# The second gate-and-up tile made whole instead of in two halves, in a hand-ordered stage

## The chip, the cores and the metric

The kernel runs on one core of a Trainium2 chip. The metric is the device time of one execution in microseconds (us), the median of several runs.

## What is computed

An input x of 2048 rows and 512 columns goes through two blocks, each behind a layer norm and with a residual. The first filters in the frequency domain, the second is a gated feed-forward network with 1376 hidden columns:

```python
def _A_ref(x, w_r, w_i):
    X = jnp.fft.rfft2(x, axes=(-2, -1))
    X = X * (w_r + 1j * w_i)
    return jnp.fft.irfft2(X, s=(S, D), axes=(-2, -1))

def _B_ref(x, w_gate, w_up, w_down):
    g = jnp.einsum("bsd,df->bsf", x, w_gate)
    u = jnp.einsum("bsd,df->bsf", x, w_up)
    return jnp.einsum("bsf,fd->bsd", _gelu(g) * u, w_down)

h = x + _A_ref(_layernorm(x), A_w_r, A_w_i)
h2 = h + _B_ref(_layernorm(h), B_w_gate, B_w_up, B_w_down)
```

## The kernel before

The Fourier transforms are matrix products with tables of cosines and sines. The 2048 rows are 16 blocks b of 128. The first part (lists START and SECOND in the code) transforms there, filters, and goes back over one axis. The stage changed here is written out by hand in the list FIRST: every name in it issues one step, and each engine works off its own steps in the order of the list. It finishes the way back for blocks 0 to 7, prepares them for the second block of the network, and makes the first two tiles of gate and up. Behind it the loop over `gate_up(n)` makes the other tiles, mixed with the products of w_down (`fill`).

The second block works in tiles: n counts (half of the rows, 128 hidden columns), and a tile's 512 columns are the rows of four pairs of blocks, (0,4), (1,5), (2,6) and (3,7), 128 columns of each block's transposed parts. Gate and up are multiplied by a scheme of seven products P0 to P6 in place of eight, and every product is done as three of high and low parts, over two halves of the contraction: six matmuls for one product, whatever its width. A tile has three PSUM banks x, y, z: 0, 1, 2 for even n, 3, 4, 5 for odd n. x takes P0, P2, P4, P5; y takes P1; z takes P3, P6.

The letters of the list, with the engine and the line of its work:

- On the way back for a block b: u, w, U (TensorE, L527: four matmuls, u and w two each), C (ACT, L853 for blocks 0 to 7, L820 for 8 to 15), V (DVE, L861; for block 3 GpSimd, L859), X (GpSimd, L884), M (TensorE, L866), O (ACT, L871), H (DVE, L876: residual), G and I (GpSimd, L880), S and A (DVE, L517 and L519: statistics). K (GpSimd, L827 to L830) unfolds a late block; U and C of blocks 8 to 15 are later needed.
- For a pair i: E (DVE, L898), Q (ACT, L911: reciprocal root), N (DVE, L903 to L905: its Newton step), R (ACT, L909: scaling, R20 is pair 2, first block), T (TensorE, L560 and L566: four transposes, T20 needs R20).
- The parts of a pair, from the transposes: s, e (ACT copies, L571 and L579), c, d, h (DVE differences, L582), k (GpSimd, L582), and the high parts a, f, i, l, n (ACT, L585) with their low parts b, g, j (DVE), m, o (GpSimd, all L588). Products P0 and P1 read a and b, P2 and P3 read f and g, P4 reads n and o, P5 reads i and j, P6 reads l and m.
- For a tile: P0 to P6 (TensorE, L163 to L165), c1, c2, c3 (ACT copies of x, L670), d1, d2, dy (DVE additions, L673), G0, G1 (ACT, L676: gelu), m0, m1 (DVE, L679: times), i0, i1 (ACT, L685: high), o0, o1 (DVE, L692: low). wh and wl load w_down (ACT and GpSimd). Tile 0 is g0, tile 1 is g1, its halves of 256 columns a and b: g0bP2 is product P2 of the second half of tile 0. g2P0 is the first product of tile 2, on bank 0, which ends the list.
- r0 to r3 (GpSimd), hc (DVE, L223) and lo1 to lo3 (GpSimd, L228) prepare the weights of tile 2.

The number behind a dot is a PSUM bank or a buffer (U15.3: bank 3, T21.7: bank 7, K9.5: row buffer 5). Waits between engines are set by the framework in the order of the list.

Of the kernel before, what the change touches and what calls it, by code (L numbers as in the profile page):

```python
# [62 lines left out]

SECOND = """
# [55 lines left out]
def kernel(  # L120
# [18 lines left out]
    o3 = out[: S // 2].rearrange("(p b) d -> p b d", b=NB // 2)  # L139
# [37 lines left out]
    k3 = ctx.enter_context(tc.tile_pool(name="k3", bufs=1))  # L177
# [57 lines left out]
    with (  # L235
# [176 lines left out]
        wh = cp.tile([P, NT, 2, 2, 2], F32, name="wh")  # L412
# [216 lines left out]
    def products(n, i=slice(0, 4)):  # L629

        w, at = gu[tiles[n][1]], slice(i.start * P, i.stop * P)

        x, y, z = places = [ps[:, 5 if k == 2 and n >= NF else 3 * (n % 2) + k, at] for k in range(3)]

        def product(o, wm, m, onto=False):
            def do():
                mm3(
                    o,
                    [
                        (  # L640
                            (w[:, 0, wm, c], w[:, 1, wm, c]),
                            tuple(cb[:, h, m, c, i].rearrange("p i n -> p (i n)") for h in range(2)),
                        )
                        for c in range(2)
                    ],
                    onto,
                )
# [12 lines left out]

    def tile_of(n, i=slice(0, 4)):

        at = slice(i.start * P, i.stop * P)
        (x, y, z), by_pe = products(n, i)
        if n not in sums:
            sums[n] = sum_tiles()
        s1, u2, u3 = (t[:, at] for t in sums[n])

        def copy(to, a):
            return lambda: act.activation(to, a, AF.Copy)  # L670

        def add(to, a, b):
            return lambda: dve.tensor_tensor(to, a, b, op=ALU.add)  # L673

        def gelu(g):
            return lambda: act.activation(g, g, AF.Gelu_apprx_tanh)  # L676

        def times(u, g):
            return lambda: dve.tensor_tensor(u, u, g, op=ALU.mult)  # L679

        def high(k, u):
            def do():
                if n not in parts_of:
                    parts_of[n] = w3.tile([P, 2, 2, 512], F32R, name="a", bufs=3)
                act.activation(parts_of[n][:, 0, k, at], u, AF.Copy)  # L685

            return do

        def low(k, u):
            def do():  # L690
                a = parts_of[n][:, :, k, at]
                dve.tensor_tensor(a[:, 1], u, a[:, 0].bitcast(F32), op=ALU.subtract)  # L692
# [99 lines left out]
    def sum_tiles():  # L792
        return [w3.tile([P, 512], F32, name=f"s{k}") for k in range(1, 4)]
# [11 lines left out]
    do = {}  # L805
# [84 lines left out]
    def pair(i):  # L890

        bs, where = slice(i, i + 5, 4), []
        r = rs2[:, bs]
        hn = [spare[1 + i // 2][:, 2 * (i % 2) + h] for h in range(2)]

        def eps_added(k):
            where.append(k)
            dve.tensor_scalar(ps[:, k, 0:2], mv2[:, bs, 1], EPS, None, op0=ALU.add)  # L898

        def newton():  # L900

# [3 lines left out]
            dve.scalar_tensor_tensor(r, t, 1.5, r, op0=ALU.add, op1=ALU.mult)  # L905

        def normed(h):
            b = i + 4 * h
            return lambda: act.activation(hn[h], gh[:, b], AF.Copy, scale=rs2[:, b : b + 1])  # L909
# [517 lines left out]
```

## Time and profile before

| what | us |
| --- | --- |
| timed runs: median of 3 | 440.44 |
| timed runs: lowest, highest | 440.41, 441.14 |
| the profiled execution | 440.5 |
| its span, first to last instruction | 438.6 |
| TensorE busy, of the span | 432.0 |
| DVE and GpSimd busy, of the span | 314.2 and 314.5 |
| ACT busy, of the span | 243.1 |

The clock granted to TensorE was 1.00 over the whole span. In the rows of the profile PE is TensorE's matmuls, PEld its loads of weights, DVE is VectorE, ACT is ScalarE, POOL is GpSimd. A row of the timeline has the start in us, the length in us, the engine, the line, the operation, what is written and read with the shapes, the number of instructions merged, and in brackets how long the engine stood idle ahead of it and what released it. Matmuls overlap, so the step from one start to the next is what a matmul takes on the path, not its own length. A row of the waits has who waited, for whom, the total in us, how often, and the longest.

### The profile page before, as it was taken

What the parts mean: (1) busy time and instruction counts of PE and PEld (TensorE: products, weight loads), DVE (VectorE), ACT (ScalarE), POOL (GpSimd) and SP (SyncE); (2) the same over time, 40 slices, a digit from 0 to 9 for tenths busy, and PEclk for the clock granted to TensorE, in tenths of its full rate; (3) what the DMA queues carried; (4) which work ended last, traced back from release to release, by engine and by line L of the source; (5) the groups of instructions that cost most, each with busy time, mean ns of one, the idle gap of its engine ahead of it and who ended that gap; (6) DMA issues with size and microseconds to landing.
All of it is one profiled execution on the core that took longest, in us unless ns stands there. A gap on an engine that the chain in (4) does not pass through costs nothing.

```text
span 438.6 us, 6625 instructions
## 1 busy us (share of the span) xinstructions
PE 432.0 (98%) x2275; PEld 366.8 (84%) x2275; DVE 314.2 (72%) x576; ACT 243.1 (55%) x502; POOL 314.5 (72%) x346
## 2 busy tenths in 40 slices
PE   8999999999999999999999999999999999999996
PEld 8999999789978777877888888888888888888885
DVE  5968896897864766368734579578677787687785
ACT  5989785799712442124432787376455653565640
POOL 6987796999859788648653944067879779787821
PEclk9999999999999999999999999999999999999999
DMA  8996904320023112112220203501212021200005
GB/s 284 400 411 85 380 10 156 128 73 24 25 96 97 49 53 92 48 50 72 72 73 24 72 25 120 169 11 62 73 48 72 28 69 49 72 24 2 0 2 192
DMA packets 23542, 41.61 MB, mean 95 GB/s; under 512 B 4178, under 2 KB 9810, under 8 KB 23380
## 3 DMA queue, kind: packets, MB, share of 16 engines
q1 hardware_dynamic: 23364, 41.05, 27.9%
q8 instruction: 18, 0.29, 0.3%
q10 hardware_dynamic: 144, 0.13, 0.1%
q14 instruction: 16, 0.13, 0.1%
HBM read 36.97 MB, written 4.20 MB: 94 GB/s over the span
## 4 chain that ended last, share of the span: by engine, by line
PE 80%; POOL 8%; DMA 5%; ACT 3%; issue 2%; DVE 1%; SPq 0%; DVEq 0%; POOLq 0%
PE ps L163 15%; PE ps L164 15%; PE ps L165 15%; PE ps L766 14%; PE ps L1105 11%; DMA gh<-in_x 3%; PE ps L527 3%; POOL z L450 3%; PE ps L866 2%; ACT dp L427 2%; DMA raw<-in_wgu 1%; PE ps L974 1%; POOL gu L157 1%; POOL pn L339 1%; PE ps L1211 1%
## 5 line engine op out<-in xcount | busy, mean ns | idle before, releaser
L163 PE MATMUL ps<-cb,gu 128*128 128x512 f32 (+1 forms) x336 | 127.2, 378 | 0.3 <-DVE a L692 0.3
L165 PE MATMUL ps<-cb,gu 128*128 128x512 f32 (+1 forms) x336 | 124.9, 372 | 0.0
L164 PE MATMUL ps<-cb,gu 128*128 128x512 f32 (+1 forms) x336 | 124.9, 372 | 0.0
L670 ACT ACTIVATE s<-ps 128x512 f32<-128x512 f32 (+1 forms) x72 | 40.4, 562 | 87.1 <-PE ps L165 86.7
L228 POOL TENSOR_TENSOR gu<-raw,gu 128x768 fp32r<-128x768 f32 (+1 forms) x42 | 61.3, 1481 | 29.0 <-DVE gu L223 16.7
L163 PEld LDWEIGHTS ps<-cb,gu 128*128 128x128 f32 x336 | 63.3, 188 | 12.3 <-issue 1.0
L164 PEld LDWEIGHTS ps<-cb,gu 128*128 128x128 f32 x336 | 63.3, 188 | 11.6 <-issue 1.0
L165 PEld LDWEIGHTS ps<-cb,gu 128*128 128x128 f32 x336 | 63.3, 188 | 11.1
L766 PE MATMUL ps<-wd,a 128*128 128x512 f32 x264 | 63.6, 393 | 0.0
L766 PEld LDWEIGHTS ps<-wd,a 128*128 128x128 f32 x264 | 49.1, 188 | 11.6 <-DVE gh L975 1.0
L679 DVE TENSOR_TENSOR ps<-ps,s 128x512 f32<-128x512 f32 (+1 forms) x48 | 31.1, 651 | 28.1 <-PE ps L165 25.3
L1112 DVE TENSOR_TENSOR gh<-ps,gh 128x512 f32<-128x512 f32 x66 | 44.2, 681 | 0.8 <-PE ps L1105 0.8
L676 ACT ACTIVATE s<-s 128x512 f32<-128x512 f32 (+1 forms) x48 | 28.4, 593 | 20.8 <-DVE s L673 20.7
L673 DVE TENSOR_TENSOR s<-ps,s 128x512 f32<-128x512 f32 (+1 forms) x48 | 30.7, 641 | 5.8 <-PE ps L165 4.7
L772 DVE TENSOR_TENSOR gh<-ps,gh 128x512 f32<-128x512 f32 x24 | 16.6, 690 | 25.3 <-PE ps L766 25.2
L508 POOL TENSOR_TENSOR wd<-wdr,wd 128x512 fp32r<-128x512 f32 x12 | 15.6, 1299 | 17.7 <-ACT wd L506 17.7
L673 DVE TENSOR_TENSOR ps<-ps,s 128x512 f32<-128x512 f32 (+1 forms) x24 | 15.7, 653 | 16.1 <-ACT s L670 15.6
L207 POOL TENSOR_TENSOR raw<-raw 128x256 f32<-128x256 f32 x16 | 11.9, 741 | 16.6 <-DMA raw<-in_wgu 14.9
L685 ACT ACTIVATE a<-ps 128x512 fp32r<-128x512 f32 (+1 forms) x26 | 13.8, 533 | 17.1 <-DVE ps L679 17.1
L1018 POOL TENSOR_TENSOR t<-mis,t 128x768 fp32r<-128x768 f32 (+1 forms) x9 | 13.3, 1481 | 13.2 <-ACT t L1016 13.2
L427 ACT ACTIVATE dp<-ps 64x520 f32<-64x520 f32 x32 | 19.1, 598 | 3.8 <-PE ps L423 3.3
L450 POOL TENSOR_TENSOR z<-t,t 128x520 f32<-128x520 f32 x15 | 19.4, 1296 | 1.0 <-DVE t L442 0.9
(182 smaller groups left out, 898.4 us busy)
## 6 DMA issues: line engine op xcount, KB each, us to landing
wt<-in_w SPq DMA_DIRECT2D x16, 520.0 KB, 7.7
raw<-in_wgu SPq DMA_DIRECT2D x32, 256.0 KB, 3.1
out<-gh SPq DMA_DIRECT2D x15, 256.0 KB, 2.0
gh<-in_x SPq DMA_DIRECT2D x7, 512.0 KB, 8.6
row<-in_x SPq DMA_DIRECT2D x12, 256.0 KB, 2.8
wdr<-in_wd SPq DMA_DIRECT2D x12, 256.0 KB, 2.6
mis<-in_wd SPq DMA_DIRECT2D x10, 256.0 KB, 2.6
a<-in_wgu SPq DMA_DIRECT2D x8, 256.0 KB, 3.1
```

The lines of the kernel that those rows point to most:

```text
L163: pe.matmul(o, lh, rh, start=(i == 0 and not onto), stop=False, skip_group_check=True)
L164: pe.matmul(o, lh, rl, start=False, stop=False, skip_group_check=True)
L165: last = pe.matmul(o, ll, rh, start=False, stop=(i == n - 1), skip_group_check=True)
L228: pooled["lo"] = pool.tensor_tensor(r[:, 1, m], t[:, m], r[:, 0, m].bitcast(F32), op=ALU.subtract)
L450: eng.tensor_tensor(z[:, :, first], t1[:, :, first], t2[:, :, first], op=ALU.add)
L670: return lambda: act.activation(to, a, AF.Copy)
L673: return lambda: dve.tensor_tensor(to, a, b, op=ALU.add)
L676: return lambda: act.activation(g, g, AF.Gelu_apprx_tanh)
L679: return lambda: dve.tensor_tensor(u, u, g, op=ALU.mult)
L766: pe.matmul(o, parts_of[tiles.index((0, f))][:, ha, i // 4, r], wds[f][:, hw, c], start=start, stop=stop)
L1105: pe.matmul(ps[:, k], w[:, hw], a[ha], start=start and hw + ha == 0, stop=hw == 1, skip_group_check=True)
L1112: by.tensor_tensor(to, o, to, op=ALU.add)
```

## The change

Tile 0 is still made in two halves, a and b. Tile 1 is made in one piece of 512 columns: 42 matmuls of 512 columns take the place of 84 of 256, and each of its steps on ACT and DVE is done once over 512 columns instead of twice over 256. The steps of tile 1 lose the letter (g1P0 for g1aP0 and g1bP0). The list FIRST is given in another order. Nothing else is changed: the other steps, the banks and buffers behind the dots and the rest of the kernel are the same.

```diff
 FIRST = """
-u0.1 u4.0 w4 C4.0 V4.2 X4 w0 C0.1 V0.3 X0 U1.2 C1.4 V1.0 X1 r0 U5.3 C5.5 V5.1 M4.1 O4.0 M0.2 O0.1 U2.3 H4 H0 X5 C2.5
-V2.3 M5.1 H5 I4 G4 O5.0 G0 I0 S4 S0 A4 A0 E0.5 U7.2 C7.1 M1.3 O1.1 g0awh H1 Q0 N0 U6.0 C6.0 V7.4 X2 U3.4 C3.5 I5 G5 S5
-M2.1 V6.3 R00 I1 G1 S1 A5 A1 R01 U9.7 C9 H2 X7 V3.1 X3 T00 a0 Q1 T01.2 s0.0 O2.1 U8.4 C8 E1.6 N1 R11 M7.0 c0 d0 f0
-U12.3 e0.1 k0 R10 H7 b0 O7.0 g0 h0 C12 X6 M6.4 H6 i0 j0 T11.1 s1.2 r1 l0 T10 c1 d1 G2 I2 M3.2 O3.1 H3 G7 a1 b1 I7 S7
-O6.0 U15.3 C15 e1.0 f1 g1 U14.5 C14 U10.4 C10 m0 k1 n1 g0aP0 g0ac1 g1aP0 l1 g0aP3 g0aP1 G3 I3 S3 A7 A3 Q3 g0aP2 I6 n0
-G6 h1 g1ac1 E3.7 N3 g1aP2 i1 R31 T31.5 g1aP1 o1 R30 T30 S2 S6 A6 A2 g1ac2 j1 E2.6 Q2 N2 o0 g1aP4 g0awl s3.6 c3 g0ac2
-g0aP4 R20 T20 a3 g1ac3 g1aP5 d3 e3.4 K9.5 m1 g0ad1 g0ac3 g0aP5 f3 b3 h3 g0ady g0aP6 i3 j3 R21 T21.7 g3 g1aP3 a2 b2
-g0bP0 g0bP1 g1bP0 K12.4 g1ad1 g1ady g1aP6 r2 l3 k3 s2.8 g1aG0 c2 d2 f2 e2.7 k2 g1bP1 g1am0 g0bc1 g2 g0bP2 g1bc1 r3 n3
-n2 o3 g1bP2 g0ad2 o2 g0aG0 g0am0 l2 m2 m3 g0bP3 h2 K8.4 g0aG1 g0am1 g0bc2 g0bP4 g1bd1 i2 j2 g1bc2 g1bP4 g1bG0 g1ad2
-g0bc3 g0bd1 g0bdy g0ai0 g0ao0 g1aG1 g1bP3 g1ai0 g1am1 g1bc3 g1bdy g0ai1 g0ao1 g0bP6 g0bd2 g1awh g1awl g1ai1 g0bG1
-g0bP5 hc g1bP6 lo1 lo2 g0bG0 g0bm0 g0bi0 g1bP5 g1bm0 g1bi0 g1bd2 g1bG1 g0bo0 U13.7 C13 lo3 g0bm1 g0bi1 U11.6 C11 g1bm1
-g1bi1 g1ao0 g0bo1 g1bo0 g1bo1 g1ao1 g2P0
+u4.0 u0.1 w4 C4.0 V4.2 X4 w0 C0.1 V0.3 U1.2 X0 C1.4 V1.0 X1 U5.3 C5.5 V5.1 M4.1 O4.0 H4 r0 M0.2 O0.1 U2.3 X5 M5.1 G4
+I4 H0 I0 G0 C2.5 V2.3 H5 S4 A4 O5.0 G5 S0 A0 U7.2 C7.1 I5 g0awh E0.5 M1.3 O1.1 X2 Q0 U6.0 C6.0 H1 G1 I1 N0 R01 U3.4
+R00 U9.7 M2.1 V7.4 T01.2 X7 S5 V6.3 X6 C3.5 T00 O2.1 s0.0 S1 A1 A5 V3.1 X3 U8.4 C9 H2 G2 c0 E1.6 d0 Q1 N1 C8 M7.0 H7
+U12.3 e0.1 f0 g0 k0 a0 b0 h0 O7.0 l0 M6.4 H6 M3.2 R11 T11.1 R10 I2 O3.1 n0 H3 I7 G7 O6.0 S7 s1.2 T10 c1 i0 j0 U10.4
+C12 l1 a1 U14.5 U15.3 d1 e1.0 m0 G3 I3 S3 A7 G6 A3 I6 f1 k1 o0 b1 g0aP0 E3.7 Q3 C14 g1 g0aP1 n1 N3 S6 r1 g0ac1 g0aP2
+h1 S2 A6 o1 R31 T31.5 R30 T30 K12.4 i1 A2 m1 K9.5 g0ac2 g0awl Q2 j1 g0ad1 E2.6 g0aP4 N2 s3.6 c3 d3 g0aP3 R20 T20 g0ac3
+g0ady g0aP6 g0aP5 a3 b3 r2 e3.4 h3 a2 b2 g0bP1 l3 i3 R21 j3 T21.7 g0aG0 g0am0 C15 f3 k3 g3 s2.8 c2 d2 C10 l2 g0bP0
+g0bc1 f2 g2 g0ad2 g1P0 g1c1 n3 e2.7 k2 n2 m2 h2 i2 j2 g1P1 o2 g1d1 g0bP2 g0bc2 g1wh g1P2 g1c2 g0bP3 g0bd1 o3 g0bP4
+g0aG1 g0am1 g1P4 m3 g0bc3 g0bdy g0bP6 g0bd2 r3 g1G0 g0ai1 g0ao1 g1c3 K8.4 g0bP5 hc g0bG0 g0bm0 g0bi0 g1P3 g1P5 g1dy
+g1P6 g0ai0 g1wl g0bG1 g0bm1 g0bi1 g1m0 g1i0 g0bo0 g1d2 g1G1 U11.6 C11 U13.7 C13 lo1 lo2 lo3 g0ao0 g2P0 g0bo1 g1m1 g1o0
+g1i1 g1o1
 """
...
-    def half(n, h):
-
-        for k, f in tile_of(n, slice(2 * h, 2 * h + 2)).items():
-            do[f"g{n}{'ab'[h]}{k}"] = f
-        if not h:
+    def part(n, i, mark):
+
+        for k, f in tile_of(n, i).items():
+            do[f"g{n}{mark}{k}"] = f
+        if mark != "b":
             down = load_d(tiles[n][1])
-            do[f"g{n}awh"] = do[f"g{n}awl"] = lambda: next(down)
+            do[f"g{n}{mark}wh"] = do[f"g{n}{mark}wl"] = lambda: next(down)
...
-    for n in range(2):
-        for h in range(2):
-            half(n, h)
+    part(0, slice(0, 2), "a")
+    part(0, slice(2, 4), "b")
+    part(1, slice(0, 4), "")
```

## The prediction

> **What bounds the kernel now.** I read the page first, for which engine is full; then the table by stretches, to see whether that holds in the stage that the list orders; then the waits of TensorE; then that stage's timeline, engine by engine.
>
> ```profile
> span 438.6 us, 6625 instructions
> PE 432.0 (98%) x2275; PEld 366.8 (84%) x2275; DVE 314.2 (72%) x576; ACT 243.1 (55%) x502; POOL 314.5 (72%) x346
> ...
> 81.20:94.20 13.00, 13.00 (x89) 10.49 (x88) 12.50 (x33) 11.61 (x28) 12.84 (x20) 1.00 0.16 49
> 95.30:108.26 12.96, 12.96 (x112) 12.96 (x111) 10.81 (x32) 12.21 (x30) 12.80 (x19) 1.00 0.08 21
> 250.00:400.00 150.00, 150.00 (x679) 124.37 (x678) 112.63 (x187) 87.15 (x164) 104.91 (x106) 1.00 0.18 60
> ...
> PE ps L163 <- DVE a L692: 0.3, 1, 0.3
> PE ps L461 <- POOL z L451: 0.3, 1, 0.3
> ```
>
> In a row of stretches the columns after the length are the busy times of PE, PEld, DVE, ACT and POOL. TensorE is at 98%, and the last two rows are its only waits from 72 us to the end. So a microsecond by which the list delays TensorE is paid in full: nothing behind the list can take it up. But in the list's stage TensorE isn't alone. From 81.20 to 94.20 DVE is busy 12.50 of 13.00 us and POOL 12.84; from 95.30 to 108.26 ACT 12.21 of 12.96. The stage is balanced: TensorE runs without waiting because the list always gives it something to do while ACT and DVE finish the next parts. The timeline of TensorE has the borders:
>
> ```profile
> 74.04 3.84 PE L527 MATMUL ps<-dis,gh 128*128 128x128 f32 x32
> ...
> 95.32 0.36 PE L163 MATMUL ps<-cb,gu 128*128 128x256 f32 x1
> 95.52 0.28 PE L164 MATMUL ps<-cb,gu 128*128 128x256 f32 x1
> ...
> 99.60 0.28 PE L165 MATMUL ps<-cb,gu 128*128 128x256 f32 x1
> ...
> 102.75 0.60 PE L560 MATMUL ps<-ident,a 128*128 128x128 f32 x4
> 103.10 0.36 PE L163 MATMUL ps<-cb,gu 128*128 128x256 f32 x1
> ...
> 108.53 0.28 PE L165 MATMUL ps<-cb,gu 128*128 128x256 f32 x1
> ...
> 110.09 0.28 PE L163 MATMUL ps<-cb,gu 128*128 128x256 f32 x1
> ...
> 117.29 1.95 PE L527 MATMUL ps<-dis,gh 128*128 128x128 f32 x16
> 119.51 0.50 PE L163 MATMUL ps<-cb,gu 128*128 128x512 f32 x1 [0.27 <-DVE a L692]
> 119.84 0.40 PE L164 MATMUL ps<-cb,gu 128*128 128x512 f32 x1
> ...
> 123.53 0.39 PE L165 MATMUL ps<-cb,gu 128*128 128x512 f32 x1
> ```
>
> By counting through the list: 74.04 is its first product, 95.32 g0aP0, 102.75 T20, 110.09 g0bP2 (the first that needs g2), 117.29 U13 and U11, 119.51 g2P0. The forecast is the shift of that 119.51.
>
> **What the whole tile saves.** Between 95.52 and 99.60 lie 34 steps of 256 columns: 0.120 us each. Between 119.84 and 123.53 lie 16 steps of 512 columns: 0.2306 us. The 84 short matmuls of tile 1 become 42 long ones: 42 x (0.240 - 0.2306) = 0.4 us less on TensorE, on the path. The 0.27 us wait may go too. The Trainium skill, "TensorE: Matmul & The Clock Gate", section "Back-to-back issue gap", gives N / 2.4 + 2.5 ns; an estimate from it is 42 x (2 x 109.2 - 215.8) = 0.1 us, so by that page joining halves is worth still less; the rows stand at 120 and 230.6 ns, and the sum uses them.
>
> ```profile
> L670 ACT ACTIVATE s<-ps 128x512 f32<-128x512 f32 x60 | 35.8, 596 | 86.4 <-PE ps L165 86.3
> L679 DVE TENSOR_TENSOR ps<-ps,s 128x512 f32<-128x512 f32 x40 | 27.9, 697 | 26.3 <-PE ps L165 25.3
> L670 ACT ACTIVATE s<-ps 128x256 f32<-128x256 f32 x12 | 4.7, 391 | 0.7 <-PE ps L165 0.5 <-DVE ps L679 0.2
> L679 DVE TENSOR_TENSOR ps<-ps,s 128x256 f32<-128x256 f32 x8 | 3.2, 423 | 1.8 <-ACT cb L585 1.8
> ```
>
> Tile 1 has seven such steps on ACT (c1, c2, c3, G0, G1, i0, i1) and seven on DVE: 7 x (2 x 391 - 596) = 1.3 us and 7 x (2 x 423 - 697) = 1.0 us less work. It all comes late in the list, behind the parts that TensorE waits for, so I cost it at nothing on the path.
>
> **What the new order costs.** A product over 512 columns reads the parts of all four pairs, so none of tile 1 can run before a2, b2, a3 and b3. In the old list nine half products of tile 1 stand ahead of g0bP2 (7 of the a half, 2 of the b half), and they are TensorE's work while pairs 2 and 3 are made ready. In the new list two whole ones stand there (g1P0, g1P1), the other five behind. I walk the four queues in list order, with durations from these rows:
>
> ```profile
> 81.20 0.42 DVE L861 TENSOR_TENSOR row<-ps,row 128x256 f32<-128x256 f32 x1 [0.40 <-ACT row L853]
> 81.55 0.74 DVE L876 SCALAR_TENSOR_TENSOR a<-a,mv,ps 128x512 f32<-128x512 f32 x1
> 94.20 0.68 DVE L588 TENSOR_TENSOR cb<-ps,cb 128x512 fp32r<-128x512 f32 x1
> 94.80 0.68 DVE L517 BATCH_NORM_STATS2 bn<-gh 128x6 f32<-128x512 f32 x1
> 96.95 0.30 DVE L519 BATCH_NORM_AGGREGATE mv<-bn 128x2 f32<-128x6 f32 x2
> 100.92 0.16 DVE L905 SCALAR_TENSOR_TENSOR rs<-ps,rs 128x2 f32<-128x2 f32 x1
> 107.03 0.88 DVE L582 TENSOR_TENSOR ps<-row,ps 128x256 f32<-128x256 f32 x2
> 108.92 0.43 DVE L679 TENSOR_TENSOR ps<-ps,s 128x256 f32<-128x256 f32 x1 [1.01 <-ACT cb L585]
> 109.26 0.68 DVE L588 TENSOR_TENSOR cb<-ps,cb 128x512 fp32r<-128x512 f32 x1
> ...
> 82.38 0.38 ACT L871 ACTIVATE t<-ps 128x256 f32<-128x256 f32 x1 [1.21 <-DVE a L876]
> 104.25 0.72 ACT L909 ACTIVATE a<-gh,rs 128x512 f32<-128x512 f32 x1
> 104.86 0.59 ACT L585 ACTIVATE cb<-ps 128x512 fp32r<-128x512 f32 x1
> 105.34 0.41 ACT L585 ACTIVATE cb<-row 128x256 fp32r<-128x256 f32 x1
> 106.64 1.28 ACT L676 ACT_TABLE_LOAD   x1
> 107.94 0.42 ACT L676 ACTIVATE s<-s 128x256 f32<-128x256 f32 x1
> 108.26 0.58 ACT L585 ACTIVATE cb<-ps 128x512 fp32r<-128x512 f32 x1
> ```
>
> A queue steps a little faster than its records last: ACT 0.61 us for a scaling (104.25 to 104.86), 0.48 for 512 columns (to 105.34); for 256 columns I take the record less the same 0.11, that is 0.28 from PSUM (0.391 above) and 0.30 to 0.33 from SBUF (0.41 and 0.42). DVE steps 0.60 for 512 columns (94.20 to 94.80), and 0.34 for 256 (81.20 to 81.55). A consumer on another engine waits for the record's end.
>
> 1. b1, which g0aP0 needs, is the DVE record of 94.20. The new list puts S7, S3, A7 and A3 ahead of it: 2 x 0.60 + 0.30 = 1.5 us on a queue without slack, so it ends at 94.88 + 1.5 = 96.4; on ACT, s1 and a1 come behind the longer run l0, O3, n0, O6, which makes 96.6. TensorE, at 95.32 before, starts g0aP0 1.3 us late. U14 waits for j0 (bank 5) at about the same place; the two delays overlap and are not added.
> 2. T20 needs R20, R20 needs N2, whose last record before ended at 101.08. The new list adds g0ad1 ahead: 101.4. R20 lasts 0.72: T20 can't start before 102.2. TensorE has five half products and two transposes until then, 5 x 0.72 + 2 x 0.44 (8 x 0.11, by the 3.84 us of the 32) = 4.5 us from 96.6: it is there at 101.1 and waits 1.1 us. Before, T20 came at 102.75 and waited for nothing, since nine half products stood between 95.32 and it, not five.
> 3. g0bP1 needs b2. On ACT from 101.4: R20, g0ac3, a3, e3, a2, that is 0.61 + 0.28 + 0.48 + 0.28 + 0.59 = 103.7; then b2 on DVE, behind h3, ends at 104.6. TensorE is there at 102.2 + 0.44 + 1.44 = 104.1: 0.5 us. T21 is then out by 105.7.
> 4. g0bP0 writes bank 0, which g0am0 of the a half still reads. Before, the list had it the other way round. g0am0 needs g0aG0, and that is the list's first gelu, so the 1.28 us load of the table stands ahead: a2 at 103.1 + 0.48 + 0.33 (l3) + 0.28 (i3) + 0.61 (R21) = 104.8, + 1.30 + 0.42 + 0.43 = 107.0. TensorE waits from 105.7, and g1P1 ends at 107.1 + 0.72 + 2 x 1.38 = 110.6.
> 5. g0bP2 needs g2. ACT goes on from 106.4 with C15, f3, s2 (0.48 each, 108.0), DVE with c2 and d2 (0.88, 108.9), ACT f2 (0.58), DVE g2 (0.68): 110.2 to 110.4 with the handings over, where it was 109.94. So g0bP2 starts at 110.5, 0.4 later than the 110.09 of before. This check doesn't hang on the other four: ahead of f2 ACT loses four 256-column steps and gains three, ahead of g2 DVE loses three and gains one, so the last pair can't come much earlier than it did.
>
> The tail decides the sum. Behind g0bP2 the old list has ten half products and U13, U11: 10 x 0.72 + 1.95 = 9.15 us, 110.09 to 119.24. The new one has five half products, five whole ones and the same U: 5 x 0.72 + 5 x 6 x 0.2306 + 1.95 = 12.5 us, 3.3 more. With 110.5 for the start, 0.2 less where the next product is pipelined behind U, and nothing for the 0.27, g2P0 comes at 122.8: **3.3 us later**.
>
> That banks of PSUM order the steps as in 4 (different columns of one bank aren't used by two engines at once) is read from rows: ACT's O5 at 82.38 waits 1.21 us for a DVE record that ended at 82.29 and reads another half of the same bank; DVE's g1am0 at 108.92 starts after the matmul in the other half of its bank ended (108.53 + 0.28). The Trainium skill, "PSUM — Partial Sum Buffer", section "PSUM bank collisions raise a hardware error", says that any two engines on one bank must be kept apart, reads too, whichever the columns. Without that rule g0bP0 would run at 105.7 and only g1P0 wait, for C15 (107.1): g2 would then gate alone, and the sum falls by 0.1 us.
>
> POOL has the same 44 us of work in both lists and I cost it at nothing; g0ady, hc (the 7 x 256 cast) and g1dy stand so on DVE that g1P6 could wait some 0.6 us behind hc: kept for the upper end.
>
> The profiled execution took 440.5 us (span 438.6, 1.9 around it): 440.5 + 3.3 = 443.8. The median of the three timed runs is 440.44, so 443.7.
>
> **The rivals.** *The parts come sooner.* ACT was not quite full. With no idle from 95.30 on, f2 could have started at 95.30 + 12.21 = 107.5, and g2 ended at 107.5 + 0.58 + 0.68 = 108.8; that gives 108.8 + 12.3 = 121.1 against 119.51, +1.6 us or 442.0. If half of ACT's 1.4 us of idle before 94.20 goes too, 441.3. For it: DVE has 2.2 us of idle in that stretch. Against: steps 2 to 4 are chains from engine to engine, not sums of work. *The other side: the order holds.* If each part lands before TensorE comes to it, only the saving is left: 0.4, the 0.27, and up to 0.4 of small steps at the start of products (0.20 instead of 0.12, as 95.32 to 95.52): -0.7 to -1.1, so 439.3 to 439.8. It decides if T20 can start by 99.8 (74.2 + 25.6 of TensorE work ahead of it) and g2 is there by 106.4 (74.2 + 32.1 of TensorE work ahead of g0bP2); for it speaks that ACT and DVE have 1.3 and 1.0 us less to do, against it that N2 alone ends after 101. *The change isn't felt*: a later wait takes up the shift. Against: TensorE has 150.00 of 150.00 us from 250 on.
>
> **How the numbers follow.** A run can tell about 0.2% (0.9 us) from no change. The walk 0.62 (442.3 to 444.9); parts sooner 0.20, nearly all of it slower by over 0.9 us (0.18); the order holds 0.14, half of it over 0.9 us faster; not felt 0.04. Faster 0.07, same 0.13, slower 0.80. The range goes from the sooner parts (441.3, and 0.1 for the spread of the runs: 441.2) to the walk with 0.6 us behind hc and 0.6 for chains a step longer than walked (444.9).
>
> **What would show it.** In the profile after: g0aP0 at about 96.6; waits of TensorE ahead of T20 (on ACT L909), ahead of g0bP1 and g0bP0 (on DVE, with the load of the table some 1.7 us earlier than 106.64); g0bP2 at 110.5; g2P0 at 122.8; the rest unchanged. Wrong: no waits of TensorE between 95 and 111, or g2P0 ahead of 120.

## Result and profile after

The median after is 444.73 us (six runs, 444.07 to 445.85), beside 440.79 of the kernel before in six runs (440.11 to 441.42): a ratio of 1.0083, 95% interval 1.0067 to 1.0100. The kernel became **3.9 us slower**; 3.3 was forecast, for 443.7 us. The profiled execution took 445.4 us, with a span of 443.6.

The page after, then the same stretch of the later loop:

```profile
span 443.6 us, 6530 instructions
PE 433.8 (98%) x2233; PEld 365.1 (82%) x2233; DVE 313.7 (71%) x569; ACT 242.9 (55%) x495; POOL 314.3 (71%) x346
...
250.00:400.00 150.00, 150.00 (x678) 124.35 (x678) 110.59 (x182) 90.26 (x169) 105.02 (x106) 1.00 0.20 65
```

There are 42 matmuls less, and seven steps less on DVE and on ACT, as the change says. TensorE is still full behind the stage, so nothing there takes up a delay. Its new waits stand in brackets in its timeline (the lines of the code are one less than before; the trace has two records for each of the four matmuls of a U, so U11 and U13 are x16):

```profile
75.01 1.16 PE L526 MATMUL ps<-dis,gh 128*128 128x128 f32 x8
...
92.35 1.10 PE L865 MATMUL ps<-row,mis 128*128 128x512 f32 x2 [0.36 <-DVE cb L587]
...
96.02 2.05 PE L526 MATMUL ps<-dis,gh 128*128 128x128 f32 x16 [0.30 <-DVE cb L587]
97.83 0.36 PE L162 MATMUL ps<-cb,gu 128*128 128x256 f32 x1
...
103.04 0.66 PE L559 MATMUL ps<-ident,a 128*128 128x128 f32 x4 [0.33 <-ACT a L908]
...
105.65 0.39 PE L163 MATMUL ps<-cb,gu 128*128 128x256 f32 x1
...
108.28 0.39 PE L162 MATMUL ps<-cb,gu 128*128 128x256 f32 x1 [1.34 <-DVE ps L678]
...
111.85 0.28 PE L162 MATMUL ps<-cb,gu 128*128 128x256 f32 x1
...
121.39 0.50 PE L162 MATMUL ps<-cb,gu 128*128 128x512 f32 x1 [0.28 <-DVE ps L672]
...
122.88 1.95 PE L526 MATMUL ps<-dis,gh 128*128 128x128 f32 x16
124.58 0.48 PE L162 MATMUL ps<-cb,gu 128*128 128x512 f32 x1
```

The list's first product starts at 75.01, where it started at 74.04 before. That part of the code is the same in both; over the profiled runs below the start lies between 73.7 and 75.1. So the stage is read by its own length, from this start to g2P0: 119.51 - 74.04 = 45.47 us before, 124.58 - 75.01 = 49.57 after, **4.10 us more**. From g2P0 to the end of the span it is 319.1 us before and 319.0 after. The whole difference is thus in the stage, and the 0.97 us by which it starts later in this execution isn't due to the change. That is also why the two spans differ by 5.0 and the medians by 3.9.

In times from the start of the stage: g0aP0 (97.83) comes at 22.8 instead of 21.3; T20 (103.04) at 28.0 instead of 28.7; g0bP0 (108.28) at 33.3; g0bP2 (111.85) at 36.8 instead of 36.05; and from g0bP2 to g2P0 it takes 12.73 us instead of 9.42. **3.3 of the 4.1 us lie behind g0bP2**, where the list has five whole products in place of five more halves.

### The profile page after: what moved, and what is told of

Read it like the earlier page. It is cut to its first block, busy times and chain, and to the rows that moved or that the text cites. A ratio compares the mean times of both kernels' runs of the same rounds, so it can differ in the third digit from the quotient of the medians.

```text
span 443.6 us, 6530 instructions
## 1 busy us (share of the span) xinstructions
PE 433.8 (98%) x2233; PEld 365.1 (82%) x2233; DVE 313.7 (71%) x569; ACT 242.9 (55%) x495; POOL 314.3 (71%) x346
## 4 chain that ended last, share of the span: by engine, by line
PE 79%; ACT 7%; POOL 5%; DVE 4%; DMA 2%; issue 2%; DVEq 0%; SPq 0%; POOLq 0%; ACTq 0%
PE ps L162 16%; PE ps L163 15%; PE ps L164 15%; PE ps L765 14%; PE ps L1104 11%; POOL z L449 3%; PE ps L526 3%; DMA raw<-in_wgu 2%; ACT dp L426 1%; PE ps L973 1%; POOL gu L156 1%; ACT ts L379 1%; PE ps L1210 1%; PE ps L865 1%; ACT ms L329 1%
## 5 line engine op out<-in xcount | busy, mean ns | idle before, releaser
L162 PE MATMUL ps<-cb,gu 128*128 128x512 f32 (+1 forms) x322 | 124.8, 388 | 1.7 <-DVE ps L678 1.3
L163 PE MATMUL ps<-cb,gu 128*128 128x512 f32 (+1 forms) x322 | 122.6, 381 | 0.0
L164 PE MATMUL ps<-cb,gu 128*128 128x512 f32 (+1 forms) x322 | 122.4, 380 | 0.0
L162 PEld LDWEIGHTS ps<-cb,gu 128*128 128x128 f32 x322 | 60.5, 188 | 15.1 <-DVE ps L678 1.6
L163 PEld LDWEIGHTS ps<-cb,gu 128*128 128x128 f32 x322 | 60.5, 188 | 12.4 <-issue 1.0
L164 PEld LDWEIGHTS ps<-cb,gu 128*128 128x128 f32 x322 | 60.5, 188 | 11.6
L678 DVE TENSOR_TENSOR ps<-ps,s 128x512 f32<-128x512 f32 (+1 forms) x46 | 30.9, 674 | 29.8 <-PE ps L164 25.6
L675 ACT ACTIVATE s<-s 128x512 f32<-128x512 f32 (+1 forms) x46 | 28.1, 610 | 20.6 <-DVE s L672 20.5
L672 DVE TENSOR_TENSOR s<-ps,s 128x512 f32<-128x512 f32 (+1 forms) x46 | 30.4, 663 | 6.9 <-PE ps L164 6.6
```

What stands on the lines that cost most here:

```text
L162: pe.matmul(o, lh, rh, start=(i == 0 and not onto), stop=False, skip_group_check=True)
L163: pe.matmul(o, lh, rl, start=False, stop=False, skip_group_check=True)
L164: last = pe.matmul(o, ll, rh, start=False, stop=(i == n - 1), skip_group_check=True)
```

## Experiments

My theory was the prediction's: a whole product of tile 1 can't run before all four pairs are ready, so its work no longer covers the making of pairs 2 and 3 and stands behind g0bP2 instead. The rivals: that the new order of the list is at fault and not the width; that the waits seen ahead of g0bP0 and g1P6 are, and go when their steps are moved; and that the later start of g0aP0 is. In all kernels below but halves_new_order and the two of the cover put back, tile 1 is whole. The stage is read as above, from the profile of each; a ratio is to runs of the kernel before taken beside that kernel's.

| kernel | median us | ratio to before (95%) | stage us | g0bP2, us from start of stage | g0bP2 to g2P0 |
| --- | --- | --- | --- | --- | --- |
| before | 440.79 | | 45.47 | 36.05 | 9.42 |
| after | 444.73 | 1.0083 (1.0067 to 1.0100) | 49.57 | 36.84 | 12.73 |
| whole_old_order | 443.93 | 1.0076 (1.0061 to 1.0091) | 48.38 | 35.92 | 12.46 |
| halves_new_order | 444.52 | 1.0097 (1.0080 to 1.0114) | 49.82 | 36.98 | 12.84 |
| gelu_later | 444.36 | 1.0086 (1.0071 to 1.0101) | 48.67 | 36.43 | 12.24 |
| old_start | 445.10 | 1.0099 (1.0083 to 1.0115) | 49.64 | 36.91 | 12.73 |
| gelu_behind_bp5 | 443.64 | 1.0055 (1.0035 to 1.0075) | 48.56 | 35.22 | 13.34 |
| cast_earlier | 447.42 | 1.0144 (1.0122 to 1.0165) | 50.85 | 36.84 | 14.01 |
| whole_repaired | 447.09 | 1.0135 (1.0113 to 1.0156) | 51.74 | 35.13 | 16.61 |
| cover_back | 448.87 | 1.0172 (1.0145 to 1.0200) | 53.77 | 39.94 | 13.83 |
| cover_back2 | 450.79 | 1.0220 (1.0203 to 1.0236) | 55.83 | 44.14 | 11.69 |
| whole_repaired2 | 443.52 | 1.0047 (1.0030 to 1.0063) | 48.28 | 35.13 | 13.15 |
| whole_covered | 447.29 | 1.0152 (1.0135 to 1.0169) | 51.01 | 35.92 | 15.09 |

**Whole tile, old order** (whole_old_order): the list of before, in which each pair of half steps of tile 1 becomes one step at the place of the second half.

```diff
...
-O6.0 U15.3 C15 e1.0 f1 g1 U14.5 C14 U10.4 C10 m0 k1 n1 g0aP0 g0ac1 g1aP0 l1 g0aP3 g0aP1 G3 I3 S3 A7 A3 Q3 g0aP2 I6 n0
-G6 h1 g1ac1 E3.7 N3 g1aP2 i1 R31 T31.5 g1aP1 o1 R30 T30 S2 S6 A6 A2 g1ac2 j1 E2.6 Q2 N2 o0 g1aP4 g0awl s3.6 c3 g0ac2
+O6.0 U15.3 C15 e1.0 f1 g1 U14.5 C14 U10.4 C10 m0 k1 n1 g0aP0 g0ac1 l1 g0aP3 g0aP1 G3 I3 S3 A7 A3 Q3 g0aP2 I6 n0 G6 h1
+E3.7 N3 i1 R31 T31.5 o1 R30 T30 S2 S6 A6 A2 j1 E2.6 Q2 N2 o0 g0awl s3.6 c3 g0ac2 g0aP4 R20 T20 a3 d3 e3.4 K9.5 m1
...
```

> Tile 1 whole, but in the old list: the steps of its a half are left out, those of its b half become the whole ones in their old places. The stage is measured from the first product of the way back to g2P0: 45.5 us before, 49.6 after. If the cover is what is lost (a whole tile can't run before all four pairs are ready, whatever the order), TensorE starts g0aP0 on time (21.3 us into the stage), then waits some 2.5 to 3 us in all ahead of T31, T20, T21 and g0bP1, and has 3.2 us more work behind g0bP2: stage 47.4 to 48.6, time +2 to +3 us over before. If only the new order is at fault and the whole tile is a gain, stage 45 to 45.3 and no time lost.

TensorE's timeline in this kernel, the rows with waits and the two ends of the tail:

```profile
99.82 0.66 PE L565 MATMUL ps<-ident,a 128*128 128x128 f32 x4 [0.63 <-ACT a L908]
101.62 0.39 PE L162 MATMUL ps<-cb,gu 128*128 128x256 f32 x1 [0.53 <-ACT s L669]
103.50 0.39 PE L162 MATMUL ps<-cb,gu 128*128 128x256 f32 x1 [0.37 <-ACT s L669]
106.45 0.39 PE L163 MATMUL ps<-cb,gu 128*128 128x256 f32 x1 [0.34 <-DVE cb L587]
...
110.62 0.28 PE L162 MATMUL ps<-cb,gu 128*128 128x256 f32 x1
...
123.08 0.50 PE L162 MATMUL ps<-cb,gu 128*128 128x512 f32 x1
```

The stage is 2.9 us longer than before with the order kept. TensorE now meets waits ahead of T31, g0aP4, g0aP5 and inside g0bP0 (its second matmul, the first that reads b2), 1.87 us in all, where 2.5 to 3 were expected and in part ahead of other steps. Nine half products (9 x 0.72 us) stood ahead of g0bP2, two whole ones (2 x 1.38) stand there now, and the waits and shorter gaps fill the place. They cost nothing by themselves: g0bP2, at 110.62, is where it was (35.9 us from the start, before 36.05). The loss is the work left behind it, 12.46 us for 9.42. The theory holds, and the order alone is not the cause; the new order adds another 1.2 us. The stage came as expected, the time a little worse: 3.3 us over before for the 2 to 3.

**Halves in the new order** (halves_new_order): tile 1 in two halves again, each whole step replaced by its two half steps side by side. What this kernel computes for tile 1 differs: both halves' first products now stand ahead of the products that add onto them in the same bank, and I take it that the second discards sums of the first, which no run shows. The instructions and their places are as meant.

```diff
...
-g0bc1 f2 g2 g0ad2 g1P0 g1c1 n3 e2.7 k2 n2 m2 h2 i2 j2 g1P1 o2 g1d1 g0bP2 g0bc2 g1wh g1P2 g1c2 g0bP3 g0bd1 o3 g0bP4
+g0bc1 f2 g2 g0ad2 g1aP0 g1bP0 g1ac1 g1bc1 n3 e2.7 k2 n2 m2 h2 i2 j2 g1aP1 g1bP1 o2 g1ad1 g1bd1 g0bP2 g0bc2 g1awh g1aP2
...
```

> The new list, but tile 1 in halves again, the two halves of each step side by side where the whole step stood. If the loss is in the order (work that stood ahead of g0bP2 now stands behind it), this stays as slow as after, or 0.3 to 0.8 us slower still, since 84 products of 0.120 us come back for 42 of 0.231: stage 49.8 to 50.4. If the width of the whole tile itself were the cost (longer steps on ACT and DVE, each holding its bank longer), it goes back to 45.5 to 46.5.

The stage is 49.82 us, 0.25 longer than after, a little less than the 0.3 to 0.8 expected. It is one profiled execution of each; their medians don't tell the two apart. So the width by itself is at most a small gain, and the loss is in where the steps stand, tile 1's products among them. Before and this kernel do the same matmuls; 4.35 us lie between them.

**The first gelu later** (gelu_later): g0aG0 and g0am0 go behind g0ad2, out of the way of g0bP0 and of the last pair's parts.

```diff
-g0ady ... T21.7 g0aG0 g0am0 C15 f3 k3 g3 s2.8 c2 d2 C10 l2 g0bP0
-g0bc1 f2 g2 g0ad2 g1P0 g1c1 ...
+g0ady ... T21.7 C15 f3 k3 g3 s2.8 c2 d2 C10 l2 g0bP0 g0bc1 f2 g2
+g0ad2 g0aG0 g0am0 g1P0 g1c1 ...
```

> As after, with g0aG0 and g0am0 moved behind g2 and g0ad2 in the list. The load of the gelu table then stands behind f2 on ACT, and g0bP0 needn't wait for g0am0. If the 1.3 us wait of TensorE ahead of g0bP0 and the load ahead of s2 are on the path, the wait goes, g2 comes some 1.6 us sooner and the stage gets 1.2 to 1.6 us shorter: 48.0 to 48.4, time -1.2 to -1.6 against after. If the other chains to g2 hide it, less than 0.4 us.

The stage gained 0.9 us, less than the 1.2 to 1.6 expected: g0bP2 came 0.4 us sooner and the tail is 0.5 shorter (g1P6 no longer waits; why is told under the tail below). The 1.34 us ahead of g0bP0 went, and another wait came, in TensorE's timeline and DVE's:

```profile
111.32 0.39 PE L162 MATMUL ps<-cb,gu 128*128 128x256 f32 x1 [1.03 <-DVE ps L678]
...
110.83 0.43 DVE L678 TENSOR_TENSOR ps<-ps,s 128x256 f32<-128x256 f32 x1 [0.70 <-ACT s L675]
```

That is g0bP2, which writes the b half of bank 0 and waits until g0am0, now later in the list, is done with the a half. So bank 0 ordered TensorE behind DVE again, though the columns differ: step 4's rule, seen at a second place. It agrees with the Trainium skill, "PSUM — Partial Sum Buffer", section "PSUM bank collisions raise a hardware error", which asks for guards by bank and not by address.

**The old start** (old_start): the list of before up to g0aP0, with C10, C14 and C15 left where the new list has them. If b1's delay counts, this takes it away.

```diff
...
-C12 l1 a1 U14.5 U15.3 d1 e1.0 m0 G3 I3 S3 A7 G6 A3 I6 f1 k1 o0 b1 g0aP0 E3.7 Q3 C14 g1 g0aP1 n1 N3 S6 r1 g0ac1 g0aP2
+O6.0 U15.3 e1.0 f1 g1 U14.5 U10.4 m0 k1 n1 n0 l1 G3 I3 S3 A7 G6 A3 I6 o0 g0aP0 E3.7 Q3 C14 g0aP1 N3 S6 g0ac1 g0aP2 h1
...
```

> As after, but with the old order up to g0aP0 (C10, C14 and C15 stay where the new list has them). b1 is on time again and g0aP0 starts at 21.3 us into the stage, not 22.8. If the delays are gates in a row, of which the latest counts, T20 still waits for R20 (N2 has as much DVE work ahead of it) and the stage gets 0 to 0.5 us shorter. If each delay adds to the next, the whole 1.5 us comes back: stage 48.0.

```profile
99.20 0.39 PE L162 MATMUL ps<-cb,gu 128*128 128x256 f32 x1 [1.26 <-ACT s L669]
102.98 0.66 PE L559 MATMUL ps<-ident,a 128*128 128x128 f32 x4 [0.32 <-ACT a L908]
```

Nothing was gained (49.64 for 49.57). The three waits before g0aP0 are gone from TensorE's timeline and g0aP0 is on time, but g0aP2 now waits 1.26 us for g0ac1, the copy out of the bank that it adds onto, and T20 stands at 28.1 us from the start, as after (28.0). Gates that stand in a row don't add up; only the last one counts.

**The first gelu behind g0bP5** (gelu_behind_bp5): as gelu_later, with g0aG0 and g0am0 moved on to the place behind hc.

```diff
...
+g1P4 m3 g0bc3 g0bdy g0bP6 g0bd2 r3 g1G0 g0ai1 g0ao1 g1c3 K8.4 g0bP5 hc g0aG0 g0am0 g0bG0 g0bm0 g0bi0 g1P3 g1P5 g1dy
...
```

> As after, with g0aG0 and g0am0 moved in the list to behind g0bP5, so that no product on bank 0 stands behind g0am0. With the two only behind g2 (gelu_later) the stage went from 49.6 to 48.7 us and TensorE waited 1.0 us for g0am0 ahead of g0bP2, on the same bank. If it is the bank that makes it wait, that 1.0 us goes too: stage 47.5 to 47.9. If the wait was for something else that g0am0 only ended last with, it stays at 48.5 or more.

g0bP2 came 1.6 us sooner than after and 0.8 sooner than before, as expected if the bank makes it wait, and there is no wait ahead of it. But the stage is 48.56, not 47.5 to 47.9; by the stage alone the other reading would have won. ACT's timeline, then TensorE's, show where it went:

```profile
113.19 1.28 ACT L675 ACT_TABLE_LOAD   x1
...
115.96 0.39 PE L162 MATMUL ps<-cb,gu 128*128 128x256 f32 x1 [0.61 <-DVE ps L672]
```

The load of the table comes with the first gelu of the list, now g0aG1. It stands ahead of g0bc3, so g0bP6 waits, and the tail is 13.34 us instead of 12.3. The load was moved, not hidden.

**The cast earlier** (cast_earlier): hc, with its weights' step r3, ahead of g0bd2, so that g1dy doesn't stand behind it.

```diff
-g0aG1 g0am1 g1P4 m3 g0bc3 g0bdy g0bP6 g0bd2 r3 g1G0 g0ai1 g0ao1 g1c3 K8.4 g0bP5 hc g0bG0 g0bm0 g0bi0 g1P3 g1P5 g1dy
+g0aG1 g0am1 g1P4 m3 g0bc3 g0bdy g0bP6 r3 hc g0bd2 g1G0 g0ai1 g0ao1 g1c3 K8.4 g0bP5 g0bG0 g0bm0 g0bi0 g1P3 g1P5 g1dy
```

> As after, with r3 and the cast hc moved ahead of g0bd2 in the list. The 0.4 to 0.5 us that TensorE waits ahead of g1P6 (for g1dy, behind the 2.0 us cast on DVE) should go: stage 49.1 to 49.2; if the wait is for the copy g1c3 or the product itself, no change.

```profile
119.37 0.36 PE L162 MATMUL ps<-cb,gu 128*128 128x256 f32 x1 [1.62 <-DVE gu L222]
```

It missed: 50.85 us. The cast writes tile 2's weights into the buffer of tile 0's, which g0bP5 still needs; put ahead of it, g0bP5 waits for the cast (and multiplies by the wrong weights, which changes that part of the computation). The 0.44 us isn't to be had this way. A list with this cast and other repairs (whole_repaired) met the same wait, 1.88 us: its stage is 51.74 us where 47.1 to 48.1 were expected, though g0bP2 came at 35.1 as forecast.

> Tile 1 whole with all the repairs together: the old order up to g0aP0 with C10 and C15, g0ad1 behind N2, the gelu and g0am0 of the a half behind g0bP5, the cast earlier. If the tail decides (12.3 us of TensorE's work behind g0bP2 where before it was 9.2), even this can't reach before: g0bP2 starts 34.8 to 35.8 us into the stage (36.1 before, since g2 is what it waits for) and the stage takes 47.1 to 48.1 against 45.5. If the waits were the whole loss, 45.0 to 45.5.

**The cover put back** (cover_back, cover_back2): the new order with tile 1 in halves, and the seven products of its a half early again, near their old places. The lines are those of cover_back2.

```diff
...
+C10 C12 l1 a1 U14.5 U15.3 C15 d1 e1.0 m0 G3 I3 S3 A7 G6 A3 I6 f1 k1 o0 b1 g0aP0 g1aP0 E3.7 Q3 C14 g1 g0aP1 n1 N3 S6 r1
+g0ac1 g0aP2 h1 g1ac1 g1aP2 S2 A6 o1 R31 T31.5 g1aP1 R30 T30 K12.4 i1 A2 m1 K9.5 g0ac2 g1ac2 g0awl Q2 j1 g0ad1 E2.6
+g0aP4 g1aP4 N2 s3.6 c3 d3 g1ad1 g0aP3 R20 T20 g0ac3 g1ac3 g0ady g0aP6 g0aP5 g1aP5 a3 b3 r2 e3.4 h3 a2 b2 g0bP1 l3 i3
...
```

> The new order of all other steps, but tile 1 in halves, its b half where the whole tile stood and its a half early, behind the a half of tile 0 (g1aP0 behind g0aP0 and so on), so that seven half products stand ahead of g0bP0 again; C10 and C15 move forward to free their banks, and the gelus and m0 of the a halves go behind g1bP4, as the bank asks for. If the cover is what the change lost, the late b1 (1.5 us) is all that is left: stage 46.3 to 47.3. If the new order of the ACT and DVE steps were the loss, it stays at 48 or more.

> The new order of the other steps, tile 1 in halves again: the b half where the whole tile stood, the seven products of the a half early (from behind g0aP0 to behind g0bP0), each with its steps on ACT and DVE; C10 and C15 forward, so that their banks are free for it. In the first try (cover_back) the gelus of the a halves stood ahead of g0bdy and the load of the table held g0bP6 up by 2.4 us; here g0aG0 stays where the new list has it. If the cover is what the change lost, TensorE still starts late by the 1.5 us of b1 and little else: stage 46.5 to 47.7. If the order of the ACT and DVE steps is the loss, 48.5 or more.

Both missed far on the slow side: 53.8 us for the stage (there g1ac1 also overwrote a buffer that pair 1 still read), then 55.8. By the bounds set ahead that speaks for the rival, the order of the ACT and DVE steps. But the a half's own steps on ACT and DVE, inserted into an order made without them, held up the others; the rows are cover_back2's:

```profile
111.48 0.39 PE L163 MATMUL ps<-cb,gu 128*128 128x256 f32 x1 [0.77 <-DVE ps L679]
115.05 0.56 PE L163 MATMUL ps<-cb,gu 128*128 128x256 f32 x1 [1.84 <-DVE ps L673]
...
127.99 0.39 PE L163 MATMUL ps<-cb,gu 128*128 128x256 f32 x1 [1.14 <-DVE ps L673]
```

So I don't count these two for either side: they put back the products and a second disturbance with them. What they show is that cover isn't products alone; every step that a product needs or releases has to be placed with it.

**The best order found for a whole tile** (whole_repaired2): the old start with its C10, C14 and C15, g0ad1 behind N2, g0aG0 and g0am0 behind g0bP5, g0aG1 and g0am1 behind g0bdy.

```diff
...
+g0aP2 h1 S2 A6 o1 R31 T31.5 R30 T30 K12.4 i1 A2 m1 K9.5 g0ac2 g0awl Q2 j1 E2.6 g0aP4 N2 s3.6 c3 d3 g0ad1 g0aP3 R20 T20
...
+g1P0 g1c1 n3 e2.7 k2 n2 m2 h2 i2 j2 g1P1 o2 g1d1 g0bP2 g0bc2 g1wh g1P2 g1c2 g0bP3 g0bd1 o3 g0bP4 g1P4 m3 g0bc3 g0bdy
+g0aG1 g0am1 g0bP6 g0bd2 r3 g1G0 g0ai1 g0ao1 g1c3 K8.4 g0bP5 hc g0aG0 g0am0 g0bG0 g0bm0 g0bi0 g1P3 g1P5 g1dy g1P6 g0ai0
...
```

> Tile 1 whole with the repairs, the cast hc where the change has it: the old order up to g0aP0 with C10 and C15, g0ad1 behind N2, g0aG0 and g0am0 behind g0bP5, g0aG1 and g0am1 behind g0bdy, so that the load of the table stands behind everything that g0bP2 and g0bP6 wait for. If the tail decides, g0bP2 starts 34.8 to 35.5 us into the stage, sooner than the 36.05 of before, and still the stage takes 47.1 to 48.0 (12.3 us behind it, up to 0.5 us of waits) against 45.5 of before. If the waits were the whole loss, 45.0 to 45.5.

```profile
109.61 0.28 PE L161 MATMUL ps<-cb,gu 128*128 128x256 f32 x1
...
119.56 0.50 PE L161 MATMUL ps<-cb,gu 128*128 128x512 f32 x1 [0.69 <-DVE ps L671]
...
122.76 0.47 PE L161 MATMUL ps<-cb,gu 128*128 128x512 f32 x1
```

This one decides for the tail. g0bP2, at 109.61, comes 35.13 us after the start, **0.9 sooner than before**, and yet the stage is 2.8 longer than before (48.3, a little over the 47.1 to 48.0 expected): a late g0bP2 is not to blame. TensorE still waits in front of it, for there stand 3.7 us less of products than before (two whole for nine halves) and g0bP2 is only 0.9 sooner. Of the 13.15 us behind it about 12.3 are products, and the rest is the wait of g1P6, whose g1dy stands behind hc and now behind g0am0 too.

**Cover from the other end** (whole_covered): U13 and U11 moved from the end of the list to banks 3 and 4 among the early products, C13 and C11 behind s2, and the end rearranged. If the tail is only too long by what it holds, 1.7 us go.

```diff
...
+O6.0 U15.3 C15 e1.0 f1 g1 U14.5 C14 U10.4 C10 m0 k1 n1 n0 l1 G3 I3 S3 A7 G6 A3 I6 o0 g0aP0 E3.7 Q3 g0aP1 U13.3 N3 S6
...
+U11.4 R20 T20 g0ac3 g0ady g0aP6 g0aP5 a3 b3 r2 e3.4 h3 a2 b2 g0bP1 l3 i3 R21 j3 T21.7 f3 k3 g3 s2.8 C13 C11 c2 d2
...
```

> whole_repaired2, with other cover for TensorE: U13 and U11 (0.89 us each, work that needs nothing of the pairs) move from the end of the list into banks 3 and 4, which a whole tile 1 leaves free until late, U13 behind g0aP1 and U11 behind g0aP3, where TensorE waited; their copies C13 and C11 go behind s2. The end of the list is put so that g1dy and g0bdy stand ahead of the cast and of the gelus. If what counts is how much of TensorE's work stands behind g0bP2, the tail shrinks from 12.3 to 10.5 us, g0bP2 stays at 35.0 to 35.6 us into the stage, and the stage takes 45.6 to 46.6 against 48.3 of whole_repaired2 and 45.5 of before: no more than 0.2% slower than before. If the waits only move (g0bP2 comes later by what was put ahead of it), 47.3 or more.

```profile
107.85 0.50 PE L162 MATMUL ps<-cb,gu 128*128 128x512 f32 x1 [0.51 <-ACT gh L819]
120.62 0.50 PE L162 MATMUL ps<-cb,gu 128*128 128x512 f32 x1 [0.66 <-DVE ps L672]
...
125.79 0.50 PE L162 MATMUL ps<-cb,gu 128*128 128x512 f32 x1 [3.50 <-DVE a L691]
```

It missed by over 4 us, and g0bP2 came at 35.9, past the 35.0 to 35.6 expected. TensorE had done all its work ahead of g2P0 by 122.3 (47.5 us from the start), and then waited 3.50 us for tile 0's low parts, which DVE was still making on bank 0. I read it so: U13 and U11 at the end of the list had been the cover for tile 0's last steps on ACT and DVE; taken away, those steps became the bound. But the end was rearranged as well (hc, with g0am0 behind it, begins 46.4 us from the start, 42.2 in whole_repaired2), and the two aren't separated. An end of the list with tile 0's gelus still earlier was not tried.

No kernel that was run beats the one before. That no order of a whole tile 1 can is not shown: the best of those run stays 2.8 us behind in the stage. One gate none of them opened sooner: b2, the last part that the first product on pairs 2 and 3 needs, ends 30.5 to 31.7 us from the start in every kernel with tile 1 whole, behind R20, which starts at 27.0 to 27.3 in all of these (27.1 before). A list that readies pair 2 sooner was not tried.

## Why the prediction was right

**Sign and mechanism.** Forecast +3.3 us, measured +3.9 in the medians and +4.10 in the stage of the two profiled executions; 444.7 lies inside the range, close to its upper end of 444.9. The mechanism was the one walked: whole_old_order loses 2.9 us by the whole tile alone, with the old order kept and g0bP2 in place, and whole_repaired2 loses 2.8 with g0bP2 sooner than before.

**The five steps**, all from the start of the stage (forecast less 74.04, measured less 75.01), with DVE's rows for j0, b1, b2, g0am0 and g2, those of the tail, and ACT's for R21 and the load:

```profile
95.55 0.42 DVE L587 TENSOR_TENSOR cb<-ps,cb 128x256 fp32r<-128x256 f32 x1
...
97.07 0.66 DVE L587 TENSOR_TENSOR cb<-ps,cb 128x512 fp32r<-128x512 f32 x1
...
104.91 0.68 DVE L587 TENSOR_TENSOR cb<-ps,cb 128x512 fp32r<-128x512 f32 x1
...
107.80 0.43 DVE L678 TENSOR_TENSOR ps<-ps,s 128x256 f32<-128x256 f32 x1 [1.87 <-ACT s L675]
...
110.92 0.69 DVE L587 TENSOR_TENSOR cb<-ps,cb 128x512 fp32r<-128x512 f32 x1 [0.67 <-ACT cb L584]
...
118.36 2.04 DVE L222 CAST gu<-raw 128x1792 fp32r<-128x1792 f32 x1
120.31 0.42 DVE L678 TENSOR_TENSOR ps<-ps,s 128x256 f32<-128x256 f32 x1
120.65 0.68 DVE L672 TENSOR_TENSOR ps<-ps,s 128x512 f32<-128x512 f32 x1
...
105.32 0.72 ACT L908 ACTIVATE a<-gh,rs 128x512 f32<-128x512 f32 x1
106.05 1.28 ACT L675 ACT_TABLE_LOAD   x1
107.35 0.42 ACT L675 ACTIVATE s<-s 128x256 f32<-128x256 f32 x1
```

1. g0aP0: forecast 22.6, measured 22.8. b1 ended 0.2 us later than forecast, at 22.7 (97.07 + 0.66 = 97.73), but no wait stands ahead of g0aP0: TensorE reached it at 97.83 straight from U14 and U15, and U14 had waited 0.30 us for j0 (95.55 + 0.42 = 95.97), the second delay that the prediction named. The two lie 0.1 us apart, so the time was right and its gate was not b1 alone; a wait of 0.36 us ahead of M3 wasn't forecast. And old_start shows that the late start costs nothing: T20 is the later gate.
2. T20: 28.2, measured 28.0, behind R20 on ACT L908 as named. The wait shown is 0.33 us and not 1.1: g0aP0 was 0.2 later, the five half products and two transposes took 4.7 us (97.83 to 102.56) and not 4.5, R20 was 0.1 sooner, and a wait is counted from the end of a record that overlaps the next step.
3. g0bP1: 30.6; its second matmul, the first that reads b2 (ended 105.59), stands at 30.6 (105.65). TensorE came there later than walked (30.4), so of the forecast wait of 0.5 us only a step of 0.21 instead of 0.12 us is left.
4. g0bP0: 33.1, measured 33.3, behind g0am0, with the gelu's load at 106.05 as named: the wait of 1.34 us is DVE L678, and that record ends at 108.23, 0.05 ahead of TensorE. The load holds ACT for 1.31 us, from R21's end at 106.04 to the gelu at 107.35. The Trainium skill, "ScalarE: Activation LUTs", section "What ACT_TABLE_LOAD costs", gives about 2.66 us for a switch with its drain; a step 4 made with that would have come about 1.4 us too late here, so the row's 1.28 was the better price.
5. g0bP2: 36.5, measured 36.8. g2 ended at 36.6 (110.92 + 0.69, forecast 36.2 to 36.4), and g1P1 kept TensorE until 111.85: the two gates lie within 0.3 us of each other, as forecast. g2's time hangs on the place of the load more than the prediction's check allowed: in gelu_later, with the load behind f2, g2 ends at 34.9, 1.0 us sooner than before, and g0bP2 moved by only 0.4 us because g0am0 then held its bank.

**The tail.** Forecast 12.3 us (12.5 less 0.2), measured 12.73. The 0.43 more is the term that the prediction put at nothing and kept for the upper end: DVE's rows show the cast hc from 118.36 to 120.40, g0bm0 behind it and then g1dy, which ends at 121.33; g1P6 starts at 121.39.

That wait isn't fixed by the list alone. GpSimd's row around hc in after, then DVE's and GpSimd's in gelu_later:

```profile
118.14 1.31 POOL L507 TENSOR_TENSOR wd<-wdr,wd 128x512 fp32r<-128x512 f32 x1
...
117.91 1.08 DVE L222 CAST gu<-raw 128x1792 fp32r<-128x1792 f32 x1
117.98 2.17 POOL L507 TENSOR_TENSOR wd<-wdr,wd 128x512 fp32r<-128x512 f32 x1
```

In after GpSimd's split of w_down began 0.22 us ahead of hc, and hc took 2.04 us; in gelu_later hc began 0.07 us ahead and took 1.08, and the split took 2.17. So it goes in all the kernels run: in the nine where hc begins inside a GpSimd instruction that lasts past its first 0.2 us, it ends 0.95 us after that instruction's end, and in the four others it takes 1.08 or 1.09. The two engines took turns here. In gelu_later g1P6 finds g1dy ready and the tail is 12.24 us: the 0.43 hangs on which of the two begins first. Moving the split (g1wl) away from hc was not tried.

The other 0.3 or 0.4 of the miss are the late ends of steps 4 and 5. So the sum's failing terms are: **g1dy behind hc, costed at 0, measured 0.43; and the chain to g0bP2, costed 0.4 us late, measured 0.8.** In a list without slack, a step of DVE that could wait 0.6 us should have been put into the sum at its walked value.

**The saving.** 0.4 us was forecast for 42 long matmuls in place of 84 short ones; halves_new_order, which changes the width with every step in its place, gives 0.25 in one execution. In it stand also the 1.3 and 1.0 us less work on ACT and DVE: that they bought nothing agrees with it, but no run separates them. The 0.27 us wait ahead of g2P0 is gone, also as said.

**The rivals.** "Parts come sooner" needed g2 by 34.8 us from the start (108.8 less 74.04); it ended at 36.6. In whole_repaired2 g2 does end at 34.8, and the stage is still 2.8 us longer than before and not 1.6. "The order holds" needed T20 by about 25.7 us from the start and g2 by about 32.3; they came at 28.0 and 36.6, and in no kernel of the table does g0bP2 come before 35.1. "Not felt" is refuted by the 319 us behind g2P0, equal in both.

## What to carry to other kernels

In a list where the engines run in lockstep, joining two halves can save little (here 0.25 us) and makes the joined work wait for the later half's inputs: count what each engine can still do while the last input is made, and what is then left behind it. Waits ahead of the last gate cost nothing by themselves, so they are compared by their latest member and not summed; the work behind that gate is paid in full. When a step is moved out of the way, look for what it covered: here the gelu's load, hc, and U13 with U11 each showed up as a new wait in another place.

## What was not expected of the hardware

In four of the experiments TensorE's granted clock fell, in three inside the stage and in whole_covered just behind it, which it does neither before nor after. The rows are stretches of cover_back2 (the granted clock is the column behind POOL's), with TensorE's timeline at the end of the fall:

```profile
110.00:115.00 5.00, 2.43 (x19) 1.99 (x17) 3.25 (x7) 3.33 (x7) 1.53 (x3) 1.00 0.11 41
115.00:120.00 5.00, 4.95 (x29) 4.96 (x29) 0.56 (x2) 1.82 (x6) 0.67 (x1) 0.66 0.00 0
...
118.17 0.41 PE L165 MATMUL ps<-cb,gu 128*128 128x256 f32 x1
118.39 0.35 PE L163 MATMUL ps<-cb,gu 128*128 128x256 f32 x1
118.58 0.28 PE L164 MATMUL ps<-cb,gu 128*128 128x256 f32 x1
118.69 0.28 PE L165 MATMUL ps<-cb,gu 128*128 128x256 f32 x1
```

The same stretches of whole_covered:

```profile
120.00:125.00 5.00, 1.66 (x6) 1.05 (x6) 3.35 (x8) 2.47 (x7) 2.70 (x3) 1.00 0.00 0
125.00:130.00 5.00, 4.21 (x12) 3.30 (x13) 4.24 (x9) 2.69 (x5) 2.82 (x2) 0.67 0.37 110
```

Behind the wait of 1.84 us in cover_back2, a matmul of 256 columns steps 0.21 us until 118.39, some 3.3 us, and 0.12 after; about 1.4 us are lost. In whole_covered, behind the 3.50, g2P0 to the end of the span takes 320.3 us instead of 319. In whole_repaired (wait 1.88) and cover_back (2.41) the clock fell too; behind the 1.62 of cast_earlier and the 1.34 of after it stayed at 1.00. So a wait can cost more than its own length. No threshold is shown: of cover_back2's four executions two have a mean granted clock of 1.00 and spans of 448.3 and 448.7 us, the other two 0.996 and 0.995 with 449.8 and 449.2. Nor need it be the length of one wait: in the 3.4 us ahead of each fall TensorE was busy 0.9 to 1.6 us, waits and work together, and in the emptiest 3.4 us of cast_earlier 1.8. The Trainium skill, "TensorE: Matmul & The Clock Gate", section "Part 1: The HAM clock gate", has the clock halved after an idle window of about 3.4 us: the half step and its 3.3 us agree, but here TensorE was not idle throughout, and the waits at the falls were 1.84 to 3.50 us long.
